# Attention and feed-forward block on one core: a second tile for a unit's finished sums, weight loads placed five slots ahead of their use, and a transposition moved ahead of the weighing

## The chip, the cores and the metric

The kernel runs on one core of a Trainium2 chip. The core has a matmul engine (TensorE, PE in the profile; PEld is its loading of weights), a vector engine (DVE), an activation engine (ScalarE, ACT), GpSimd (POOL) and a queue engine (SyncE, SP) that here issues nearly all transfers. Each works through its own instructions in order and waits on the others by semaphores. The metric is the time of one execution in microseconds (us) on the device; less is better.

## The reference

A pre-normalized attention block and a SwiGLU feed-forward block, in float32, for 2048 tokens of width 640, with 32 heads of 20 and a hidden width of 1728:

```python
qkv = (x @ wqkv).reshape(B, S, 3, H, Dh).transpose(2, 0, 3, 1, 4)   # x: layernormed A_x
scores = jnp.einsum("bhqd,bhkd->bhqk", q, k) * (Dh ** -0.5)
p = softmax(scores, axis=-1)
o = jnp.einsum("bhqk,bhkd->bhqd", p, v)
h = A_x + o.transpose(0, 2, 1, 3).reshape(B, S, D) @ wo
y = layernorm(h)
out = h + (silu(y @ w_gate) * (y @ w_up)) @ w_down
```

## The kernel before

The program has three parts: the projections to queries, keys and values (up to about 324 us in the profile), the attention, and the output projection with the feed-forward. The order of the instructions on each engine is that in which the Python code writes them; a framework adds the semaphores and gives out buffers of named tiles in rotation (`bufs` says how many a tile has). An instruction that writes a tile waits until the last reader of that buffer's former content is done.

The attention is 32 units: 8 groups of 4 heads (g) times 4 chunks of 512 queries (c), `u = 4 * g + c`. Each unit runs over 16 key tiles of 128 keys (`kt`). A step, here also called a slot, is one key tile of one unit; its work is written in the order of the string `ORDER = "WxnSmSsMXs"`:

- `s`, `S`: a product of scores of 128 keys with 512 queries for one head (L1290, PE) and its exponential (L1296, ACT). Four in a step. Their results go through four PSUM banks in turn (`ps_one`).
- `W`: weighing. The probabilities of the key tile two steps back are multiplied with the values (L1300, PE) into the bank `acc`. After the last key tile, `row_sums` copies `acc` into the tile `o` on ACT (L1310), and SP takes the row with the sums of probabilities out of it (`r<-o`, L1313).
- `m`, `M`, `x`, `X`: products of scores for a later unit (L261, L289), of which DVE takes maxima (L267, L298) for that unit's softmax.

The query tile `q_stk` has two rows beside those of each head's queries, into which the negative maximum is written before the unit starts, as a high and a low part; the score product then subtracts it. When the last maximum of unit v is there, DVE puts them together (`neg`, L309) and `closing[v]` is set to two steps later. For most units (`early_end`) the maxima go by way of POOL, DVE and DRAM (`m_d`). For unit 1 and for each last unit of a group (u = 3, 7, ..., 31, called late units here) `max_finish` does it: PE transposes `neg` (L345) into a bank of the `ps_one` rotation, ACT and DVE split it into the tile `m2` (`m` in the profile's names), and SP copies it into the query tile in four transfers (`q_stk<-m`, L352). The last maximum of a late unit comes at key tile 11 of the unit before it, `closing` is key tile 13, and its scores start three steps after that.

The rest of a finished unit is handled in the next one: DVE takes the reciprocal of `r` (L1321) at key tile 4, SP sends it through DRAM (`r_d<-r`, L1323) and spreads it over the partitions (`rb<-r_d`, L1329), POOL scales `o` at key tile 9 (L1335), and SP stores `o` to `o_d` in four transfers at key tile 13 (L1338; 11 in the last group). SP also loads queries three units ahead at key tile 6, the next group's keys in the second unit of a group and its values in the third (L164, L181; at key tiles 8, 10, 12 and 14).

In the `W` of nearly every step (all but key tiles 3 and 4, from unit 1 on) one task of `prepare_weights` is run. It makes the sums and the high and low parts of the feed-forward weights that the third part needs, on POOL, and stores them in DRAM (`w_d`, `d_d`, `j_d`). For a block of weights the tasks are: `load` (SP loads `raw`, L1128 or L1182), empty tasks, `sums` (L1140 to L1145), and pieces (L1108, L1109). Each task, also an empty one, first issues the stores of the piece before it (`store()`, L1099), which wait for POOL. `raw` is two tiles.

Of the kernel before, what the change touches and what calls it, by code (L numbers as in the profile page):

```python
# [9 lines left out]
F32 = mybir.dt.float32  # L10
# [7 lines left out]
P = 128  # L18
# [7 lines left out]
CH = 512  # L26
# [27 lines left out]
def tile_block(ctx: ExitStack, tc: tile.TileContext, x, wqkv, wo, wg, wu, wd, out):  # L54
# [1036 lines left out]
    def prepare_weights():  # L1091


        stores, count = [], [0]

        def store():
            while stores:
                dst, t = stores.pop(0)
                nc.sync.dma_start(dst.bitcast(F32), t.bitcast(F32))  # L1099

        def staged(n):

            count[0] += 1
            t = stages[count[0] % 2][:, count[0] // 2 % 5, : 2 * n]
            return t.rearrange("p (i n) -> p i n", i=2), t

        def part(src, hi, lo):
            nc.gpsimd.tensor_copy(hi, src)  # L1108
            nc.gpsimd.tensor_tensor(out=lo, in0=src, in1=hi.bitcast(F32), op=ALU.subtract)  # L1109

        def nothing():
            store()

        def block(f):

            raw, src = [], {}
            whole = f < NF - 1

            def load():
                store()  # L1120
                for i, m in enumerate((wg, wu)):
                    if whole or i == 0:
                        raw.append(pc.tile([P, ND, P], F32, name="raw", tag="o_t"))
                    if whole:
                        dst, cols = raw[i], m[:, f * P : (f + 1) * P]
                    else:
                        dst, cols = raw[0][:, :, i * LASTW : (i + 1) * LASTW], m[:, f * P :]
                    nc.sync.dma_start(dst, cols.rearrange("(k p) n -> p k n", p=P))  # L1128
                src["A11"], src["A12"] = raw[0][:, 0:2], raw[0][:, 2:4]
                if whole:  # L1130
                    src["A22"] = raw[1][:, 2:4]

            def sums(i):
                store()
                g, u = raw
                t = pc.tile([P, 2, 2, P], F32, name="sums", tag="z2")
                x, y = t[:, 0], t[:, 1]
                tt = nc.gpsimd.tensor_tensor
                if i == 0:
                    tt(out=x, in0=u[:, 0:2], in1=u[:, 2:4], op=ALU.add)  # L1140
                    tt(out=y, in0=x, in1=g[:, 0:2], op=ALU.subtract)
                    src["S1"], src["S2"] = x, y
                else:
                    tt(out=x, in0=g[:, 0:2], in1=u[:, 0:2], op=ALU.subtract)
                    tt(out=y, in0=g[:, 2:4], in1=src["S2"], op=ALU.subtract)  # L1145
                    src["S3"], src["S4"] = x, y

            def unit(kind):
                store()
                t, whole_t = staged(2 * P)  # L1150
                t = t.rearrange("p i (k n) -> p i k n", k=2)
                part(src[kind], t[:, 0], t[:, 1])
                stores.append((w_d[f][:, UNITS.index(kind)], whole_t))

            def last():
                store()
                t = staged(2 * P)[0].rearrange("p i (k n) -> p i k n", k=2)
                for i, r in enumerate(raw):
                    part(r[:, ND - 1], t[:, 0, i], t[:, 1, i])
                n = len(raw)  # L1160
                stores.append((
                    w_d[f][:, 7].rearrange("p (i k n) -> p i k n", i=2, k=2)[:, :, :n], t[:, :, :n]
                ))

            if not whole:
                return [load, nothing, nothing] + [lambda k=k: unit(k) for k in ("A11", "A12")] + [last]
            return (
                [load, nothing, nothing, lambda: sums(0), lambda: sums(1)]
                + [lambda k=k: unit(k) for k in ("A11", "A12")] + [last]
                + [lambda k=k: unit(k) for k in ("A22", "S2", "S1", "S3", "S4")]  # L1170
            )

        def rows(fs, together):

            raw, src = {}, {}

            def load():
                store()
                for f in fs:
                    raw[f] = pc.tile([P, D], F32, name="raw", tag="o_t")  # L1180
                    if f < NF - 1:
                        nc.sync.dma_start(raw[f], wd[f * P : (f + 1) * P, :])  # L1182
                    else:
                        for i in range(2):
                            nc.sync.dma_start(
                                raw[f][i * LASTW : (i + 1) * LASTW, :], wd[f * P :, :]
                            )
                    for i in range(2):
                        src[f, i] = raw[f][:, i * HALF : (i + 1) * HALF]

            def sums(i):
                store()
                b11, b12, b21, b22 = (src[f, k] for f in fs for k in range(2))
                t = pc.tile([P, 2, HALF], F32, name="sums", tag="z2")
                x, y = t[:, 0], t[:, 1]
                tt = nc.gpsimd.tensor_tensor
                if i == 0:
                    tt(out=x, in0=b12, in1=b11, op=ALU.subtract)
                    tt(out=y, in0=b22, in1=x, op=ALU.subtract)
                    src["T1"], src["T2"] = x, y  # L1200
                    src["B11"], src["B21"], src["B22"] = b11, b21, b22
                else:
                    tt(out=x, in0=b22, in1=b12, op=ALU.subtract)
                    tt(out=y, in0=b21, in1=src["T2"], op=ALU.subtract)
                    src["T3"], src["T4"] = x, y

            def piece(name, dst):
                store()
                t, whole = staged(HALF)
                part(src[name], t[:, 0], t[:, 1])  # L1210
                stores.append((dst, whole))

            tasks = [load, nothing, nothing]
            if together:
                tasks += [lambda: sums(0), lambda: sums(1)]
                for i, (_, name, _) in enumerate(SEVEN):
                    tasks.append(lambda i=i, n=name: piece(n, j_d[fs[0] // 2][:, i]))
            else:
                for f in fs:
                    for i in range(2):  # L1220
                        tasks.append(lambda f=f, i=i: piece((f, i), d_d[f][:, i]))
            return tasks

        tasks = []
        for f in range(NF):
            tasks += block(f)
        for f in range(0, NF, 2):
            if f < NF - 2:
                tasks += rows((f, f + 1), True)
            if f in d_d:  # L1230
                tasks += rows((f, f + 1), False)
        return tasks + [store]
# [73 lines left out]
            )  # L1306

    def row_sums(acc, *queues):
        o = pc.tile([P, CH], F32, name="o", bufs=1)
        nc.scalar.activation(o, acc, AF.Copy)  # L1310
        r = pc.tile([P, 16], F32, name="r")
        for j in range(G):
            queues[j % len(queues)].dma_start(  # L1313
                r[32 * j : 32 * j + 32, :],
                o[32 * j + DH : 32 * j + DH + 1, :].rearrange("r (p f) -> r p f", p=32),
            )
        return o, r
# [63 lines left out]
    for u in range(NU):  # L1381
# [4 lines left out]
        for kt in range(NT):  # L1386
# [5 lines left out]
            for op in order:  # L1392
# [7 lines left out]
                elif op in "sS":  # L1400
                    scores(u, kt, heads[op == "S"].pop(0), probs)
                else:
                    if len(todo) == 2:
                        weigh_next()
                    for v, at in closing.items():
                        if at == now[0] and not early_end(v):
                            max_finish(v)
                        elif at == now[0]:
                            store_maxima(v)
                        elif at == now[0] - 3 and early_end(v):  # L1410
                            send_maxima(v)
                    if extra:
                        extra.pop(0)()
                    if preparing and u and kt not in (3, 4):
                        preparing.pop(0)()
                    if now[0] == (NU - NC) * NT + 8:
                        unit_ring, last_ring = weight_rings()
                        unit_ring.fill()
                        last_ring.fill()
            todo.append((u, kt, probs))  # L1420
            if kt == 6 and u + 3 < NU:
                load_queries(u + 3)
            if kt == 10 and u == 0:
# [599 lines left out]
```

## Time and profile before

| | us |
|---|---|
| runs timed (three) | 2020.04, 2023.31, 2024.53; median 2023.31 |
| profiled execution | 2016.94 |
| its span, first to last instruction | 2015.1 |
| granted TensorE clock | 1.00 |

The profiled execution's own time is 1.84 us above its span and 0.3% below the median of the timed runs. In the profile's rows, a line of code is L with its number, `out<-in` are tiles by name, and a bracket at a row's end gives the time that the engine was idle ahead of it and what ended that. Slots of `SPq` are SP issuing a transfer; how long the transfer itself takes is not in that row.

### The profile page before, as it was taken

What the parts mean: (1) busy time and instruction counts of PE and PEld (TensorE: products, weight loads), DVE (VectorE), ACT (ScalarE), POOL (GpSimd) and SP (SyncE); (2) the same over time, 40 slices, a digit from 0 to 9 for tenths busy, and PEclk for the clock granted to TensorE, in tenths of its full rate; (3) what the DMA queues carried; (4) which work ended last, traced back from release to release, by engine and by line L of the source; (5) the groups of instructions that cost most, each with busy time, mean ns of one, the idle gap of its engine ahead of it and who ended that gap; (6) DMA issues with size and microseconds to landing.
All of it is one profiled execution on the core that took longest, in us unless ns stands there. A gap on an engine that the chain in (4) does not pass through costs nothing.

```text
span 2015.1 us, 41996 instructions
## 1 busy us (share of the span) xinstructions
PE 1986.7 (99%) x14792; PEld 1262.6 (63%) x14792; DVE 1607.9 (80%) x2873; ACT 1433.6 (71%) x2833; POOL 782.8 (39%) x1147
## 2 busy tenths in 40 slices
PE   8999999999999999999999999999999999999998
PEld 6989996444344444444444444455588888888888
DVE  5687778999899899999999998975488666676667
ACT  4677778999999999999999999987633222212221
POOL 6564423343352444443500001011155444844455
PEclk9999999999999999999999999999999999999999
DMA  7787563442534544435412122222258655974642
GB/s 237 261 255 253 176 210 86 128 152 93 182 112 126 159 123 145 150 134 183 152 55 73 45 80 58 79 63 62 62 195 286 228 175 171 356 254 158 206 146 93
DMA packets 197066, 310.50 MB, mean 154 GB/s; under 512 B 51368, under 2 KB 85480, under 8 KB 195832
## 3 DMA queue, kind: packets, MB, share of 16 engines
q1 hardware_dynamic: 190264, 284.21, 43.7%
q0 software_dynamic: 6496, 23.60, 4.0%
q8 instruction: 118, 1.93, 0.4%
q14 instruction: 92, 0.75, 0.1%
q10 hardware_dynamic: 96, 0.00, 0.0%
HBM read 208.11 MB, written 99.19 MB: 152 GB/s over the span
## 4 chain that ended last, share of the span: by engine, by line
PE 85%; DMA 4%; DVE 1%; POOL 1%; issue 1%; SPq 1%; ACT 0%; ACTq 0%; POOLq 0%; DVEq 0%
PE acc L1300 23%; PE ps_a L1486 15%; PE ps_one L1290 11%; PE ps_max L289 8%; PE ps_b L1580 8%; PE ps_one L667 6%; PE ps_max L261 6%; PE ps_max L228 2%; PE ps_max L1021 2%; PE ps_b L1021 1%; DMA q_stk<-q_d 1%; DMA halves<-j_d 1%; DMA w_d<-stage 1%; DMA k_stk<-k_d 0%; DMA o_d<-o 0%
## 5 line engine op out<-in xcount | busy, mean ns | idle before, releaser
L1296 ACT ACTIVATE probs<-ps_one 128x512 f32<-128x512 f32 x2048 | 1048.8, 617 | 45.3 <-PE ps_one L1290 33.5
L267 DVE TENSOR_REDUCE found<-ps_max 128x1 f32<-128x512 f32 x980 | 630.7, 685 | 88.6 <-PE ps_max L261 70.5
L1290 PE MATMUL ps_one<-q_stk,k_stk 62*128 62x512 f32 x2048 | 578.6, 428 | 1.1 <-DMA q_stk<-m 0.7
L1300 PE MATMUL acc<-probs,v_stk 128*32 128x512 f32 x4096 | 545.2, 604 | 0.2
L289 PEld LDWEIGHTS ps_max<-k_stk,q_stk 60*128 60x128 f32 x984 | 181.7, 185 | 407.2 <-DVE found L267 390.3
L261 PE MATMUL ps_max<-k_stk,q_stk 60*128 60x512 f32 x980 | 393.2, 422 | 0.0
L298 DVE TENSOR_REDUCE found<-ps_max 128x2 f32<-128x512 f32 x492 | 335.7, 683 | 3.1 <-PE ps_max L289 3.1
L289 PE MATMUL ps_max<-k_stk,q_stk 60*128 60x256 f32 x984 | 324.5, 330 | 4.7 <-ACTq L304 4.6
L1290 PEld LDWEIGHTS ps_one<-q_stk,k_stk 62*128 62x128 f32 x2048 | 303.0, 184 | 26.1 <-ACT probs L1296 21.3
L1701 DVE TENSOR_TENSOR tmp<-ps_a,tmp 128x512 f32<-128x512 f32 x208 | 141.2, 689 | 119.5 <-PE ps_a L1486 93.9
L250 DVE TENSOR_REDUCE mx<-ps_max 128x2 f32<-128x512 f32 x288 | 180.5, 685 | 64.0 <-PE ps_max L228 60.0
L261 PEld LDWEIGHTS ps_max<-k_stk,q_stk 60*128 60x128 f32 x980 | 181.0, 185 | 50.4 <-DVE found L298 23.5
L240 ACT ACTIVATE ps_max<-ps_max 128x512 f32<-128x512 f32 x288 | 151.7, 584 | 46.2 <-PE ps_max L228 43.6
L1580 PE MATMUL ps_b<-halves,yp 128*128 128x320 f32 x1032 | 179.3, 308 | 1.9 <-POOL yp L102 1.2
L1580 PEld LDWEIGHTS ps_b<-halves,yp 128*128 128x128 f32 x1032 | 165.1, 188 | 18.5 <-POOL yp L102 1.5
L1486 PE MATMUL ps_a<-t,units 128*128 128x512 f32 x624 | 162.5, 396 | 0.0
L1300 PEld LDWEIGHTS acc<-probs,v_stk 128*32 128x32 f32 x4096 | 80.6, 108 | 129.4 <-issue 120.7
L1486 PE MATMUL ps_a<-z,units 128*128 128x512 f32 x516 | 133.9, 394 | 0.0
L102 POOL TENSOR_TENSOR yp<-y,yp 128x256 fp32r<-128x256 f32 x96 | 60.2, 627 | 188.0 <-ACT yp L101 180.3
L1486 PEld LDWEIGHTS ps_a<-t,units 128*128 128x128 f32 x624 | 112.6, 188 | 18.5
L1335 POOL TENSOR_TENSOR o<-o,rb 128x512 f32<-128x512 f32 x31 | 39.8, 1285 | 195.6 <-DMA q_stk<-q_d 109.8
L1585 DVE TENSOR_TENSOR h<-ps_b,h 128x320 f32<-128x320 f32 x248 | 110.1, 481 | 7.1 <-PE ps_b L1580 5.6
(220 smaller groups left out, 2975.9 us busy)
## 6 DMA issues: line engine op xcount, KB each, us to landing
units<-w_d SPq DMA_DIRECT2D x186, 256.0 KB
w_d<-stage SPq DMA_DIRECT2D x106, 256.0 KB
halves<-j_d SPq DMA_DIRECT2D x70, 320.0 KB
j_d<-stage SPq DMA_DIRECT2D x42, 320.0 KB
k_stk<-k_d SPq DMA_DIRECT2D x64, 160.0 KB
q_stk<-q_d SPq DMA_DIRECT2D x64, 160.0 KB
raw<-k_d SPq DMA_DIRECT2D x62, 160.0 KB
raw<-q_d SPq DMA_DIRECT2D x54, 160.0 KB
```

What stands on the lines that cost most here:

```text
L240: nc.scalar.activation(ps, ps, AF.Relu)
L250: nc.vector.tensor_reduce(mx[:, b, :, t, kc], ps.rearrange("p (j n) -> p j n", j=2), axis=AX.X, op=ALU.max,)
L261: nc.tensor.matmul(ps, queries[u][rows, pair, t * P : (t + 1) * P], keys[u // NC][rows, pair, kc * CH : (kc + 1) * CH], start=True, stop=True,
L267: nc.vector.tensor_reduce(found_of(u)[:, b, pair, t, kc : kc + 1], ps, axis=AX.X, op=ALU.max)
L289: nc.tensor.matmul(ps[:, b * CH // 2 : (b + 1) * CH // 2], queries[u][rows, pair, t * P : (t + 1) * P], keys[u // NC][rows, pair, first : ...
L298: nc.vector.tensor_reduce(found_of(u)[:, :, pair, t, column], ps.rearrange("p (b n) -> p b n", b=2), axis=AX.X, op=ALU.max,)
L1290: nc.tensor.matmul(ps, keys[u // NC][rows, p, kt * P : (kt + 1) * P], queries[u][rows, p, :], start=True, stop=True,)
L1296: nc.scalar.activation(probs[p][:, b, :], ps, AF.Exp, scale=scale)
L1300: nc.tensor.matmul(acc[32 * j : 32 * j + 32, :], values[u // NC][:, kt, j * VW : j * VW + 32], probs[j // 2][:, j % 2, :], start=(kt == 0) ...
L1486: nc.tensor.matmul(ps.rearrange("p (t n) -> p t n", t=TPC), w[k][:, i], z[k][:, :, j], start=(first and m == 0), stop=(last and m == len(n ...
L1580: nc.tensor.matmul(ps, a, b, start=(n == 0), stop=(n == len(pairs) - 1))
L1701: add = lambda out, ps, x: nc.vector.tensor_tensor(out=out, in0=ps, in1=x, op=ALU.add)
```

## The change

Three edits. `row_sums` gets a second buffer for `o`. In `prepare_weights` each load is followed by four empty tasks instead of two, so the first use of what it loads is five tasks later instead of three; the list grows from 269 to 315 tasks and ends in unit 23 instead of unit 20. And `max_finish` of a late unit is called at the end of the step ahead of `closing`, after that step's last scores, where it was called within the `W` of the step `closing`, after its weighing; it also comes ahead of the loads that stand at that step's end.

```diff
@@ prepare_weights: block, rows
-                return [load, nothing, nothing] + [lambda k=k: unit(k) for k in ("A11", "A12")] + [last]
+                return [load] + [nothing] * 4 + [lambda k=k: unit(k) for k in ("A11", "A12")] + [last]
             return (
-                [load, nothing, nothing, lambda: sums(0), lambda: sums(1)]
+                [load] + [nothing] * 4 + [lambda: sums(0), lambda: sums(1)]
...
-            tasks = [load, nothing, nothing]
+            tasks = [load] + [nothing] * 4
@@ row_sums
-        o = pc.tile([P, CH], F32, name="o", bufs=1)
+        o = pc.tile([P, CH], F32, name="o", bufs=2)
@@ the steps
                     for v, at in closing.items():
-                        if at == now[0] and not early_end(v):
-                            max_finish(v)
-                        elif at == now[0]:
+                        if at == now[0] and early_end(v):
                             store_maxima(v)
...
             todo.append((u, kt, probs))
+            for v, at in closing.items():
+                if at == now[0] + 1 and not early_end(v):
+                    max_finish(v)
             if kt == 6 and u + 3 < NU:
                 load_queries(u + 3)
```

The order on PE around the transposition for unit 3, before. The rows of L1290 are the scores of the running unit, those of L261 and L289 products for later maxima, L1300 the weighing:

```order
L261 MATMUL ps_max<-k_stk_5609,q_stk 128x512
L289 MATMUL ps_max<-k_stk_5609,q_stk 128x256
L1290 MATMUL ps_one<-q_stk,k_stk_145 128x512
L1300 MATMUL acc<-probs,v_stk_146 32x512 x4
L345 MATMUL ps_one<-ident,neg 16x128
L289 MATMUL ps_max<-k_stk_5609,q_stk 128x256
L1290 MATMUL ps_one<-q_stk,k_stk_145 128x512
```

The same place after:

```order
L261 MATMUL ps_max<-k_stk_5609,q_stk 128x512
L289 MATMUL ps_max<-k_stk_5609,q_stk 128x256
L1290 MATMUL ps_one<-q_stk,k_stk_145 128x512
L345 MATMUL ps_one<-ident,neg 16x128
L1300 MATMUL acc<-probs,v_stk_146 32x512 x4
L289 MATMUL ps_max<-k_stk_5609,q_stk 128x256
L1290 MATMUL ps_one<-q_stk,k_stk_145 128x512
```

The transposition (L345) has changed places with the weighing products of one step.

The order on SP in unit 10, from the spreading of the reciprocals to the copies of unit 11's maxima (L352), before. `w_d` are stores of pieces, `raw` loads of weights, `v_stk` loads of values:

```order
L1329 DMA rb<-r_d 128x1x512
L1099 DMA w_d_83<-stage 128x512 x2
L1128 DMA raw<-in_B_w_gate 128x5x128
L1128 DMA raw<-in_B_w_up 128x5x128
L164 DMA q_stk<-q_d_60 40x1024
L164 DMA q_stk<-q_d_60 20x1024
L164 DMA q_stk<-q_d_60 40x1024
L164 DMA q_stk<-q_d_60 20x1024
L181 DMA v_stk_5610<-v_d 128x4x96 x2
L1099 DMA w_d_84<-stage 128x512
L181 DMA v_stk_5610<-v_d 128x4x96
L352 DMA q_stk<-m_11443 1x8x128 x4
```

And after, from the loads of queries on:

```order
L164 DMA q_stk<-q_d_60 20x1024
L1099 DMA w_d_82<-stage 128x512 x2
L181 DMA v_stk_5610<-v_d 128x4x96
L1099 DMA w_d_82<-stage 128x512 x2
L181 DMA v_stk_5610<-v_d 128x4x96
L1099 DMA w_d_82<-stage 128x512
L1128 DMA raw<-in_B_w_gate 128x5x128
L1128 DMA raw<-in_B_w_up 128x5x128
L352 DMA q_stk<-m_11389 1x8x128 x4
L181 DMA v_stk_5610<-v_d 128x4x96
L1338 DMA o_d<-o 20x512 x4
```

Before, the store ahead of the copies (`w_d_84`) is of the block whose load stands a few rows above it. After, all stores ahead of the copies are of a block (`w_d_82`) that was loaded in the unit before; the next block's load stands right ahead of the copies, and one load of values has come behind them.

## The prediction

> **What bounds the kernel now.** I read the page first, then the busy times by stretch, then what ScalarE (ACT) waited for, then the timelines around each wait. The first line is the page's busy times; the second is busy time of the engines in the stretch in which the attention runs undisturbed by other matmuls (PE, PEld, DVE, ACT, POOL in that order, with instruction counts), then the granted clock and the DMA share.
>
> ```profile
> PE 1986.7 (99%) x14792; PEld 1262.6 (63%) x14792; DVE 1607.9 (80%) x2873; ACT 1433.6 (71%) x2833; POOL 782.8 (39%) x1147
> ...
> 328.00:1342.00 1014.00, 1008.18 (x7676) 424.47 (x7672) 919.01 (x1569) 993.11 (x1958) 305.76 (x506) 1.00 0.38 114
> ```
>
> All three edits act between 328 and 1342 us. There ACT is busy 993.11 of 1014 us (98%) and PE's modelled time fills the stretch too: the two run in step, four exponentials against four score products per key tile. ACT works through its instructions in order, so what it idles here nothing gives back. These are all its idle times of 0.4 us or more in the stretch, in the timeline of ACT (start, length, instruction, and in brackets the idle time ahead of it and what ended it):
>
> ```profile
> 529.78 0.60 ACT L1310 ACTIVATE o<-acc 128x512 f32<-128x512 f32 x1 [2.60 <-DMA o_d<-o]
> ...
> 665.52 0.60 ACT L1310 ACTIVATE o<-acc 128x512 f32<-128x512 f32 x1 [1.70 <-DMA w_d<-stage]
> 698.38 2.06 ACT L1296 ACTIVATE probs<-ps_one 128x512 f32<-128x512 f32 x4 [1.14 <-PE ps_max L261]
> 735.31 0.60 ACT L1310 ACTIVATE o<-acc 128x512 f32<-128x512 f32 x1 [1.44 <-DMA o_d<-o]
> ...
> 936.72 0.60 ACT L1310 ACTIVATE o<-acc 128x512 f32<-128x512 f32 x1 [0.43 <-DMA j_d<-stage]
> 969.06 2.06 ACT L1296 ACTIVATE probs<-ps_one 128x512 f32<-128x512 f32 x4 [0.64 <-PE ps_max L261]
> ```
>
> Four are the copy of a unit's sums into `o` (L1310), two the first exponential of a unit. That they are lost for good shows in the distance between these copies, one per unit of 16 key tiles:
>
> ```profile
> 493.60 0.63 ACT L1310 ACTIVATE o<-acc 128x512 f32<-128x512 f32 x1
> ...
> 563.46 0.63 ACT L1310 ACTIVATE o<-acc 128x512 f32<-128x512 f32 x1
> ...
> 596.89 0.63 ACT L1310 ACTIVATE o<-acc 128x512 f32<-128x512 f32 x1
> ```
>
> From 563.46 to 596.89 a unit takes 33.43 us, 2.09 per key tile. From 493.60 to 529.78 it took 36.18, which is 2.75 more and holds the idle 2.60; the next (to 563.46) took 33.68 and recovered nothing.
>
> **Edit 1, two tiles for the finished sums.** With one `o`, the copy for unit u waits until unit u-1's four stores to `o_d` have landed. The stores of the first case, between key loads, in the timeline of SP:
>
> ```profile
> 521.16 2.13 SPq L164 DMA_DIRECT2D k_stk<-k_d  x4
> 523.87 2.95 SPq L1338 DMA_DIRECT2D o_d<-o  x4
> 527.51 1.88 SPq L164 DMA_DIRECT2D k_stk<-k_d  x4
> ```
>
> SP came to the stores only at 523.87, behind a key load, issued the last of them by 526.82, and ACT went on at 529.78. (The other three cases name neighbouring transfers as what ended the wait; it is the same instruction at the same place.) With a second tile the copy needs the stores of u-2, a unit (33.4 us) older, and these were late by at most 2.6. The wait is gone in all four cases: 2.60 + 1.70 + 1.44 + 0.43 = 6.17 us. I take the idle times; the unit's excess of 2.75 against 2.60 says that up to about 0.2 more per case could come back, which I keep for the range. The edit adds no instruction. What is late next in these places is SP's row `r<-o`, behind four key loads: they end at 529.39, and DVE's reciprocals need `r`. For an undisturbed unit:
>
> ```profile
> 426.80 0.63 ACT L1310 ACTIVATE o<-acc 128x512 f32<-128x512 f32 x1
> 427.46 3.42 SPq L1313 DMA_DIRECT2D r<-o  x4
> 435.34 0.24 DVE L1321 RECIPROCAL r<-r 128x16 f32<-128x16 f32 x1
> ```
>
> The reciprocal comes 8.54 us after the copy starts. In unit 5 the copy would start at 527.18, `r<-o` be issued from 529.39 to about 532.8 (3.42, as here), and the reciprocal come at 535.7: 2.9 us are left for the landing. A small copy's landing can be read below as 1.29, so nothing waits.
>
> **Edit 2, loads two slots further ahead.** It adds 46 empty slots, which hold no computing, and moves the preparation's end from unit 20 to unit 23; the weights are read from unit 28 on, so no end moves. Its worth lies in the two first exponentials above. The timelines of POOL, SP and PE for the first (unit 11):
>
> ```profile
> 677.89 0.46 SPq L1128 DMA_DIRECT2D raw<-in_B_w_gate  x1
> ...
> 687.52 0.72 POOL L1140 TENSOR_TENSOR sums<-raw 128x256 f32<-128x256 f32 x1 [18.65 <-DMA raw<-in_B_w_up]
> ...
> 692.86 0.34 SPq L1099 DMA_DIRECT2D w_d<-stage  x1
> 693.24 0.44 SPq L181 DMA_DIRECT2D v_stk<-v_d  x1
> 693.78 2.81 SPq L352 DMA_DIRECT2D q_stk<-m  x4
> 697.88 0.47 PE L1290 MATMUL ps_one<-q_stk,k_stk 62*128 62x512 f32 x1 [0.73 <-DMA q_stk<-m]
> ```
>
> The raw weights took 9.63 us to land (677.89 to 687.52); POOL then made sums, scaled `o` and split the first piece, which SP could store at 692.86: 14.97 us from load to store. The maxima's four copies (L352) stood behind that store. They were issued by 696.59 and the score ran at 697.88, which makes 1.29 us to land; in unit 3, shown below, they start 5.9 us ahead of the score, here 4.1. Before, six slots lie between a load and its first store, 12.5 us at 2.09, and in units 10 and 18 that store stands just ahead of the copies. After, wherever such a store stands ahead of a late unit's copies, at least eight key tiles lie between it and its load (unit 22, whose pieces need no sums; ten in units 2, 14 and 18), 16.7 us: more than 14.97. So both waits go: 1.14 + 0.64 = 1.78 us. Taken at the other end, if they only change place, it is 0. I take 1.78, because eight key tiles cover the longest case. What the loads are moved past: in units 17 to 22 they now stand in key tile 2, on SP behind `r<-o` and ahead of `r_d<-r` and `rb<-r_d`, where their issue costs about 1 us (two of 0.46, by the row above) and their 640 KB travel with `rb`. On POOL the sums that wait for a load now mostly stand behind the scaling of `o` of that unit instead of ahead of it. Both are covered by the room until the scaling's key tile 9, seven key tiles or 14.6 us after the load; if that cover is gone, `o` is stored later, and the second tile hides that.
>
> **Edit 3, the transposition ahead of the weighing.** The late unit 3, which is not disturbed:
>
> ```profile
> 416.29 0.25 DVE L309 TENSOR_REDUCE neg<-found 128x16 f32<-128x96 f32 x1
> ...
> 416.85 1.06 PE L1300 MATMUL acc<-probs,v_stk 128*32 128x512 f32 x8
> ...
> 417.85 0.28 PE L345 MATMUL ps_one<-ident,neg 128*16 128x128 f32 x1
> 418.05 0.38 PE L289 MATMUL ps_max<-k_stk,q_stk 60*128 60x256 f32 x1
> ...
> 418.18 0.25 ACT L101 ACTIVATE m<-ps_one 16x128 fp32r<-16x128 f32 x1
> ...
> 418.45 2.84 SPq L352 DMA_DIRECT2D q_stk<-m  x4
> 418.59 8.36 ACT L1296 ACTIVATE probs<-ps_one 128x512 f32<-128x512 f32 x16 [0.16 <-PE ps_one L1290]
> 424.35 0.49 PE L1290 MATMUL ps_one<-q_stk,k_stk 62*128 62x512 f32 x1
> ```
>
> PE pays 0.2 us for the transposition (417.85 to 418.05) on either side of the eight weighing products, and ACT's copy into `m` stays behind the same four exponentials, so it starts at 418.18 as before. The maximum is ready at 416.54, 0.31 us before PE comes to the place at 416.85. The term is 0; its ends are a gain of the 0.16 that ACT idles at 418.59 and a loss of 0.2, nine times each: -1.4 to +1.8. The margin of the copies is 424.35 - (421.29 + 1.29) = 1.77 us, and one load of values (0.44 at 693.24) now stands behind the copies instead of ahead: good for a backlog, no loss, since those values are for the next group of heads.
>
> **Sum.** -6.17 - 1.78 + 0 = -7.95 us on the profiled execution's 2016.94 gives 2009.0. The three timed runs before have the median 2023.31, 0.3% above the profiled one, so I take the same 7.95 off that: 2015.4.
>
> **Rivals.**
> Rival 1, late units' copies late elsewhere. In unit 10 after the change the raw load (640 KB) stands right ahead of the copies. The nearest case, in unit 6 before:
>
> ```profile
> 549.78 0.45 SPq L1128 DMA_DIRECT2D raw<-in_B_w_gate  x1
> ...
> 555.11 2.82 SPq L352 DMA_DIRECT2D q_stk<-m  x4
> ...
> 556.15 0.74 POOL L1140 TENSOR_TENSOR sums<-raw 128x256 f32<-128x256 f32 x1 [7.41 <-DMA raw<-in_B_w_up]
> 561.01 0.49 PE L1290 MATMUL ps_one<-q_stk,k_stk 62*128 62x512 f32 x1
> ```
>
> The load landed in 6.37 us, during the copies, and PE did not wait. Against it: SP reaches unit 10's load about one key tile later than this one. If again two units wait, edits 2 and 3 bring nothing: 2023.31 - 6.17 = 2017.1. The Trainium skill ("DMA: Bandwidth & Descriptors", section "Queues, rings and completion order") says that each DMA engine takes descriptors of one issuing queue in ring order, so the copies could not pass such a load. By that rule, with a landing of 9.63 us and then the usual 1.29, unit 10's successor would wait about 0.6 us (the load stands two key tiles or 4.4 us ahead of the copies and these 5.9 ahead of the score, 10.3 in all), and the sum would be 2016.0; the case of unit 6, where the load landed in time, neither shows nor excludes it.
>
> Rival 2, no change: the backlog moves to DVE. If `r` lands late, DVE, in order, holds the maxima behind the reciprocal, and PE and ACT follow. For it: SP's backlog itself is not removed by a second tile. Against it: 2.9 us of room above, and these are all of DVE's waits in the stretch, none for `r`:
>
> ```profile
> DVE found L267 <- PE ps_max L261: 68.4, 260, 1.2
> DVE found L298 <- PE ps_max L289: 3.1, 3, 1.7
> DVE h L1027 <- PE ps_max L1021: 2.0, 1, 2.0
> DVE m L102 <- ACT m L101: 0.2, 1, 0.2
> ```
>
> If the four waits came back whole there, only 1.78 would be won: 2021.5.
>
> Rival 3, slower: PE is held at the transposition by the maximum, with the eight weighing products queued behind it, and ACT and DVE starve. It decides when DVE runs later than now by more than 0.31 us; to outweigh 7.95 and reach +0.2% (4.05) it takes 12.0 / 9 = 1.33 us of waiting in each of nine late units. DVE behind by three more of its reductions would make 3 x 0.68 - 0.31 = 1.73 each, 15.6 in all, and 2031.0. Against it: the 68.4 us in which DVE itself waits for PE say that it has room. A reduction's size:
>
> ```profile
> 436.87 0.68 DVE L298 TENSOR_REDUCE found<-ps_max 128x2 f32<-128x512 f32 x1
> ```
>
> **How the numbers follow.** Chances: the forecast 0.62, rival 1 0.19, rival 2 0.13, rival 3 0.06. The forecast and rival 1 (-0.31%) are faster by more than 0.2%, about what a measurement here can tell from no change (the three runs before span 4.5 us); rival 2 (-0.09%) is within it. That gives 0.81, 0.13, 0.06. The range: at the low end the forecast less the kept 0.8 (four times 0.2), less 1.4 for edit 3, and less some 2 for the scatter of a median of runs that span 4.5: 2011. At the high end rival 2: 2021.5. The forecast's own range is 2011 to 2018.
>
> **What the profile after would show.** Right: no idle time ahead of L1310, so that copies of sums stand 33.4 to 33.7 us apart from unit 2 to unit 23; no wait of PE or ACT at the first score of units 11 and 19; the stretch that ends at 1342 now ends about 8 us sooner, with what follows unchanged in length. Wrong: a wait of DVE at L1321, of PE at L345 with the maximum as its end, or a score that waits for `q_stk<-m`. The forecast fails most easily if PE, not ACT, sets the key tile's 2.09 us, so that a freed ACT finds no scores to work on.

## The result, and the profile after

The changed kernel's median is 2009.93 us over six runs, the kernel before's 2022.64 over six; the ratio is 0.9945, with a 95% interval of 0.9927 to 0.9962. A second comparison, further below, gave 0.9958 (0.9944 to 0.9971). The change makes the kernel faster by about half a per cent. The profiled executions are 2016.94 before and 2008.45 after, 8.49 us apart. Two executions of the kernel before, of 3357 and 3631 us, and one of the divided copy below, of 3631 us, ran in a slow state and are left out of the ratios.

All that ACT waited for after the change, between 328 us and the end of the undisturbed attention (1333 us; 1342 before), as who waited for what, total, times, longest:

```profile
ACT probs L1296 <- PE ps_one L1290: 3.1, 13, 0.3
```

The copy L1310 is no longer in this list, and no wait is longer than 0.3 us. The busy times of the stretch (PE, PEld, DVE, ACT, POOL; then the granted clock, the DMA share and GB/s):

```profile
328.00:1333.00 1005.00, 1004.68 (x7667) 423.48 (x7668) 918.62 (x1569) 991.74 (x1956) 305.69 (x506) 1.00 0.38 115
```

ACT's work is what it was (991.74 us, before 993.11 in a stretch cut at slightly other places); its idle time has shrunk, from 20.9 us to 13.3. The timeline of ACT where before had the longest stall:

```profile
493.00 0.63 ACT L1310 ACTIVATE o<-acc 128x512 f32<-128x512 f32 x1
...
526.40 0.63 ACT L1310 ACTIVATE o<-acc 128x512 f32<-128x512 f32 x1
...
560.11 0.63 ACT L1310 ACTIVATE o<-acc 128x512 f32<-128x512 f32 x1
593.53 0.63 ACT L1310 ACTIVATE o<-acc 128x512 f32<-128x512 f32 x1
```

The copies stand 33.40, 33.71 and 33.42 us apart; the 36.18 of before is gone. SP, however, still comes to the stores of `o` in that unit only behind key loads:

```profile
518.75 2.98 SPq L164 DMA_DIRECT2D k_stk<-k_d  x8
522.62 2.01 SPq L1338 DMA_DIRECT2D o_d<-o  x4
```

The last store is issued by 524.63, behind eight key loads, and the copy starts at 526.40, 1.77 us later. Before, 0.36 us lay between them (526.82, and 527.18 for the copy without its wait), so the stores do come somewhat earlier. That alone would not have been enough: in the run with edits 2 and 3 and one tile, below, the same order left ACT waiting 1.13 us at this copy. The second tile makes the landing of these stores irrelevant.

Unit 11, whose first score had waited, in the timelines of SP, POOL and PE:

```profile
681.58 0.45 SPq L1128 DMA_DIRECT2D raw<-in_B_w_gate  x1
682.08 1.07 SPq L1128 DMA_DIRECT2D raw<-in_B_w_up  x1
685.68 2.82 SPq L352 DMA_DIRECT2D q_stk<-m  x4
...
687.67 0.73 POOL L1140 TENSOR_TENSOR sums<-raw 128x256 f32<-128x256 f32 x1 [7.43 <-DMA raw<-in_B_w_up]
691.57 0.49 PE L1290 MATMUL ps_one<-q_stk,k_stk 62*128 62x512 f32 x1
```

The copies go out at 685.68, 5.89 us ahead of the score, as in an undisturbed unit before. The raw load right ahead of them landed in 6.09 us (681.58 to 687.67), and the score did not wait. Last, the transposition of unit 3:

```profile
415.44 0.25 DVE L309 TENSOR_REDUCE neg<-found 128x16 f32<-128x96 f32 x1
...
416.21 0.28 PE L345 MATMUL ps_one<-ident,neg 128*16 128x128 f32 x1
416.42 1.07 PE L1300 MATMUL acc<-probs,v_stk 128*32 128x512 f32 x8
417.41 0.38 PE L289 MATMUL ps_max<-k_stk,q_stk 60*128 60x256 f32 x1
417.48 0.25 ACT L101 ACTIVATE m<-ps_one 16x128 fp32r<-16x128 f32 x1
...
417.94 0.60 ACT L1296 ACTIVATE probs<-ps_one 128x512 f32<-128x512 f32 x1 [0.21 <-PE ps_one L1290]
```

PE transposes 1.2 us ahead of the next key tile's products instead of directly ahead of them, and ACT's copy into `m` still waits its turn behind the exponentials. ACT idles 0.21 us there, before 0.16.

### The profile page after: what moved, and what is told of

It is laid out like the page before. It is cut to its first block, busy times and chain, and to the rows that moved or that the text cites. A ratio compares the mean times of both kernels' runs of the same rounds, so it can differ in the third digit from the quotient of the medians.

```text
span 2006.6 us, 41982 instructions
## 1 busy us (share of the span) xinstructions
PE 1983.5 (99%) x14792; PEld 1261.6 (63%) x14792; DVE 1606.8 (80%) x2873; ACT 1433.0 (71%) x2833; POOL 784.4 (39%) x1147
## 3 DMA queue, kind: packets, MB, share of 16 engines
q8 instruction: 118, 1.93, 0.4%
## 4 chain that ended last, share of the span: by engine, by line
PE 88%; DMA 2%; DVE 1%; POOL 1%; issue 1%; ACT 0%; SPq 0%; DVEq 0%; ACTq 0%; POOLq 0%
PE acc L1300 25%; PE ps_a L1487 15%; PE ps_one L1290 12%; PE ps_max L289 9%; PE ps_b L1581 8%; PE ps_max L261 7%; PE ps_one L667 7%; PE ps_max L228 2%; PE ps_max L1021 2%; PE ps_b L1021 1%; DMA o_t<-o_d 0%; DMA units<-w_d 0%; DMA halves<-j_d 0%; DMA t_d<-kept 0%; PE ps_max L1056 0%
## 5 line engine op out<-in xcount | busy, mean ns | idle before, releaser
L1290 PE MATMUL ps_one<-q_stk,k_stk 62*128 62x512 f32 x2048 | 577.4, 428 | 1.1 <-DVE m L102 0.9
L1300 PE MATMUL acc<-probs,v_stk 128*32 128x512 f32 x4096 | 545.2, 604 | 0.0
L289 PEld LDWEIGHTS ps_max<-k_stk,q_stk 60*128 60x128 f32 x984 | 181.8, 185 | 407.2 <-DVE found L267 400.3
L261 PE MATMUL ps_max<-k_stk,q_stk 60*128 60x512 f32 x980 | 392.7, 422 | 0.0
L289 PE MATMUL ps_max<-k_stk,q_stk 60*128 60x256 f32 x984 | 324.1, 329 | 0.0
L1290 PEld LDWEIGHTS ps_one<-q_stk,k_stk 62*128 62x128 f32 x2048 | 303.1, 184 | 25.3 <-ACT probs L1296 19.5
L261 PEld LDWEIGHTS ps_max<-k_stk,q_stk 60*128 60x128 f32 x980 | 181.0, 185 | 50.2 <-DVE found L298 21.9
L1300 PEld LDWEIGHTS acc<-probs,v_stk 128*32 128x32 f32 x4096 | 80.6, 108 | 127.6 <-issue 118.5
```

Source lines behind the costliest of these rows:

```text
L261: nc.tensor.matmul(ps, queries[u][rows, pair, t * P : (t + 1) * P], keys[u // NC][rows, pair, kc * CH : (kc + 1) * CH], start=True, stop=True,
L289: nc.tensor.matmul(ps[:, b * CH // 2 : (b + 1) * CH // 2], queries[u][rows, pair, t * P : (t + 1) * P], keys[u // NC][rows, pair, first : ...
L1290: nc.tensor.matmul(ps, keys[u // NC][rows, p, kt * P : (kt + 1) * P], queries[u][rows, p, :], start=True, stop=True,)
L1300: nc.tensor.matmul(acc[32 * j : 32 * j + 32, :], values[u // NC][:, kt, j * VW : j * VW + 32], probs[j // 2][:, j % 2, :], start=(kt == 0) ...
```

## The experiments

Each was timed in turn with the kernel before on the same chip. The idle times are those of the run's own profiled execution.

| run | median | before beside it | ratio (95%) |
|---|---|---|---|
| edit 1 alone | 2009.75 | 2020.48 | 0.9951 (0.9938 to 0.9965) |
| edit 2 alone | 2016.04 | 2020.48 | 0.9976 (0.9965 to 0.9986) |
| edit 3 alone | 2020.64 | 2020.48 | 0.9998 (0.9987 to 1.0008) |
| edits 2 and 3 | 2017.33 | 2020.48 | 0.9982 (0.9973 to 0.9990) |
| before again | 2021.50 | 2020.77 | 1.0002 (0.9990 to 1.0013) |
| all, one empty slot | 2015.31 | 2020.77 | 0.9974 (0.9960 to 0.9988) |
| all, copy divided | 2015.00 | 2020.77 | 0.9973 (0.9962 to 0.9984) |
| all, high part on DVE | 2010.83 | 2020.77 | 0.9947 (0.9929 to 0.9965) |
| all, copy on DVE | 2011.35 | 2020.05 | 0.9962 (0.9949 to 0.9974) |
| the change again | 2009.77 | 2020.05 | 0.9958 (0.9944 to 0.9971) |

**The three edits apart.** My theory was that the stalls are separate and each edit takes its own; the rival, that the place of the loads is the root of all of them.

Edit 1 alone:

```diff
-        o = pc.tile([P, CH], F32, name="o", bufs=1)
+        o = pc.tile([P, CH], F32, name="o", bufs=2)
```

> Edit 1 alone: `o` has two tiles, loads and transposition as before. Theory (the stalls are separate, each edit takes its own): the four idle times of ACT ahead of L1310 go, those at the first score of units 11 and 19 stay within about 1 us of 1.14 and 0.64; 6 to 7 us less than before in the profiled execution, ratio about 0.997. Rival (the load's place is the root of all stalls): also no wait at L1310, since the second tile hides it, so this run does not tell the two apart by its time. Rival (the backlog moves to DVE): DVE waits for `r` at L1321 in the same units and the time is within 2 us of before.

All of ACT's waits from 330 us on in this run:

```profile
ACT probs L1296 <- PE ps_max L261: 1.8, 2, 1.2
ACT probs L1296 <- PE ps_one L1290: 1.0, 5, 0.3
```

Nothing waits at L1310, and the two first scores of units 11 and 19 wait their 1.8 us as before. By the list of stalls this is as expected; by the time it is more: 10.7 us between the medians where 6 to 7 were expected. Why is the subject of a part below. (Ahead of 330 us stands one more wait, of 1.45 us, which is also taken up there.)

Edit 2 alone:

```diff
-                [load, nothing, nothing, lambda: sums(0), lambda: sums(1)]
+                [load] + [nothing] * 4 + [lambda: sums(0), lambda: sums(1)]
```

(and the two like it in blocks and rows)

> Edit 2 alone: four empty slots behind each load, one `o` tile, transposition as before. Theory: units 11 and 19 no longer wait for their maxima, but ACT still waits at L1310 wherever SP comes late to the stores of `o`, some 3 to 6 us in all in other units; 1 to 4 us less than before, ratio 0.998 to 0.9995. Rival (the load's place is the root): with sums that never hold POOL, the stores of `o` are in time and nothing waits at L1310; about 8 us less than before, ratio about 0.996, as the full change.

```profile
528.91 0.60 ACT L1310 ACTIVATE o<-acc 128x512 f32<-128x512 f32 x1 [1.55 <-DMA o_d<-o]
664.85 0.60 ACT L1310 ACTIVATE o<-acc 128x512 f32<-128x512 f32 x1 [1.92 <-DMA k_stk<-k_d]
...
1102.82 0.60 ACT L1310 ACTIVATE o<-acc 128x512 f32<-128x512 f32 x1 [0.75 <-PE ps_max L261]
```

These, at the copies of units 5, 9 and 22, are its waits at L1310; the first scores of units 11 and 19 no longer wait. SP in unit 9, ahead of the second:

```profile
655.45 4.01 SPq L164 DMA_DIRECT2D k_stk<-k_d  x8
660.04 1.74 SPq L1338 DMA_DIRECT2D o_d<-o  x4
662.30 1.91 SPq L164 DMA_DIRECT2D k_stk<-k_d  x4
```

Here POOL is not late (in unit 9 it had scaled `o` by 648.28) and the stores of `o` still stand behind eight key loads. So the loads' place is not the root of the waits in units 5 and 9; there it is the order of SP's queue in the second unit of a group. The other two waits at L1310, those of units 11 and 17, do not come in this run, nor in edits 2 and 3 together. For unit 11 the rows of before and of this run show why: before, POOL scaled `o` only at 724.80, behind sums that had waited for their load, and SP came to the stores at 730.35; here POOL scaled it at 717.33 and SP came at 725.18. So the rival is right for that wait and wrong for those of units 5 and 9. The 1.78 us at the first scores and the 1.87 at units 11 and 17 make 3.65 us of the 4.4 between the medians.

Edit 3 alone:

```diff
-                        if at == now[0] and not early_end(v):
-                            max_finish(v)
...
             todo.append((u, kt, probs))
+            for v, at in closing.items():
+                if at == now[0] + 1 and not early_end(v):
+                    max_finish(v)
```

> Edit 3 alone: the late units' maxima transposed ahead of the weighing, one `o` tile, two empty slots. Theory: PE pays its 0.2 us on either side, so all six stalls stay, and the time is that of before within 1.5 us. Because the copies now stand ahead of one load of values, the waits of units 11 and 19 may shrink by up to 0.5 each. Rival (the place of the transposition matters by itself): 3 us or more either way.

The time is that of before within 0.1%. At the first score of unit 11 ACT waits 0.47 us instead of 1.14 and at that of unit 19 no wait is listed, as expected of copies that stand ahead of one load of values. Its waits at L1310 sum to 8.7 us, more than the 6.17 of the execution I had worked from: 6.5 us in units 5, 9 and 17 (3.76, 1.21 and 1.49), none in unit 11, and four of 0.40 to 0.72 at other copies. That not all of the six stalls stayed where they were was not expected.

Edits 2 and 3, the change with one `o` tile:

```diff
-        o = pc.tile([P, CH], F32, name="o", bufs=2)
+        o = pc.tile([P, CH], F32, name="o", bufs=1)
```

> The full change without edit 1: one `o` tile, loads five slots ahead, transposition ahead of the weighing. Theory: as edit 2 alone, 1 to 4 us less than before; ACT waits at L1310 are back, 3 to 6 us in all. Rival (the load's place is the root): as the full change, about 8 us less than before, no wait at L1310.

```profile
ACT o L1310 <- DMA o_d<-o: 3.5, 2, 2.4
ACT o L1310 <- DMA k_stk<-k_d: 3.0, 1, 3.0
```

6.5 us of waiting at L1310 are back, and 7.5 us in time against the full change's medians of 2009.8 to 2009.9, which come from other jobs; by the ratios it is 5 to 7.5. The waits stand in units 5 and 9, and a new one in unit 22:

```profile
1099.38 2.34 SPq L1338 DMA_DIRECT2D o_d<-o  x4
...
1104.64 0.60 ACT L1310 ACTIVATE o<-acc 128x512 f32<-128x512 f32 x1 [2.38 <-DMA o_d<-o]
```

There the moved raw loads (1097.66 to 1099.33) stand right ahead of the stores, which needed until 1104.64 to free the tile. So edit 2 without edit 1 took two of the old waits away, and in both of its runs one came at unit 22, where before had none. Edit 1 carries the change. What edits 2 and 3 add to it is the 1.8 us of waits at the first scores, which lies within the intervals of the timed runs (0.9951 alone, 0.9945 and 0.9958 with them).

**Why the gain is over 8 us.** The kernel before, unchanged:

> The kernel before, unchanged, profiled once more. Theory: the length of ACT's waits at L1310 follows the landing of transfers and differs from one execution to the next; the profiled execution of before, 2016.94, was one of the fastest of its kernel (all runs 2017.1 to 2026.1, median 2020.5), so this profile shows the same places with more than 7.95 us of idle in all, by about as much as its time is above 2017. Rival (the difference between executions lies elsewhere, in the projections or the feed-forward): the idle is again about 8 us and another stretch is longer.

This profiled execution took 2021.22 us, where the first took 2016.94. All of ACT's idle times of 0.4 us or more from 500 to 1000 us:

```profile
531.62 0.60 ACT L1310 ACTIVATE o<-acc 128x512 f32<-128x512 f32 x1 [4.21 <-DMA k_stk<-k_d]
535.15 2.07 ACT L1296 ACTIVATE probs<-ps_one 128x512 f32<-128x512 f32 x4 [0.98 <-PE ps_one L1290]
537.92 20.63 ACT L1296 ACTIVATE probs<-ps_one 128x512 f32<-128x512 f32 x40 [0.71 <-PE ps_one L1290]
...
668.21 0.60 ACT L1310 ACTIVATE o<-acc 128x512 f32<-128x512 f32 x1 [0.83 <-DMA w_d<-stage]
701.01 2.07 ACT L1296 ACTIVATE probs<-ps_one 128x512 f32<-128x512 f32 x4 [1.11 <-PE ps_max L261]
738.12 0.60 ACT L1310 ACTIVATE o<-acc 128x512 f32<-128x512 f32 x1 [1.63 <-DMA o_d<-o]
940.21 0.60 ACT L1310 ACTIVATE o<-acc 128x512 f32<-128x512 f32 x1 [1.07 <-DMA j_d<-stage]
972.81 2.07 ACT L1296 ACTIVATE probs<-ps_one 128x512 f32<-128x512 f32 x4 [0.89 <-PE ps_max L261]
```

The six places are the same six. They sum to 9.74 us, where the first execution had 7.95: the waits were 1.79 us longer. The two idle times that follow the longest within 7 us, 1.69 us together, are of another kind. The busy times there (PE, PEld, DVE, ACT, POOL; then the granted TensorE clock) and two of PE's weighings:

```profile
533.00:535.00 2.00, 2.00 (x12) 0.68 (x6) 0.04 (x1) 1.17 (x3) 1.84 (x6) 0.50 0.07 15
537.00:539.00 2.00, 2.00 (x24) 0.92 (x16) 1.25 (x3) 1.29 (x4) 1.84 (x5) 1.00 0.12 45
...
532.46 1.93 PE L1300 MATMUL acc<-probs,v_stk 128*32 128x512 f32 x8
538.40 1.06 PE L1300 MATMUL acc<-probs,v_stk 128*32 128x512 f32 x8
```

The granted clock fell to 0.50 at about 530 us, while PE stood still because ACT waited, and was back at 1.00 by 537. In between, the eight products of a weighing took 1.93 us instead of 1.06, and ACT waited for scores. From copy to copy this unit took 35.43 us (531.62 to 567.05); the first execution, whose clock stayed at 1.00 behind its wait of 2.60, took 33.68 there. So a wait can cost a second time after it has ended. The third difference is an idle time of 1.33 us at 328 us, at the attention's start, where the granted clock was also 0.50. It comes with two tiles too: the run of edit 1 alone has one like it, 1.45 us at a clock of 0.53. (The three sum to 4.81 us and not to the 4.28 between the two executions, since the second began its attention 1.2 us sooner.)

The rest of the gain in the timed runs goes along with the clock. Of the 73 executions of the kernel before in the experiments, only nine had a mean granted clock of 0.999 or 1.000, with a median of 2017.0 us; the other 64, at 0.993 to 0.998, have 2020.8. Of the changed kernel's eleven, nine had 0.999 or 1.000, with a median of 2009.5. At that clock the two kernels are 7.6 us apart, close to the list of stalls. Taken by tiles, 15 of 106 executions with one `o` tile (before, edit 2, edit 3, edits 2 and 3) reach that clock, and 13 of 16 with two (edit 1 alone, the change); where edit 1 was timed in turn with the kernel before, it was four of 5 against one of 27. How much of the difference is the clock itself, and how much longer waits in the same executions, the times alone do not tell.

So the theory holds in part: the waits do differ from one execution to the next, but longer waits are less than half of the difference between the two profiled executions. The rival, that another stretch is longer, has the 1.33 us at the attention's start for it. What neither named is the granted clock. What makes it fall is not settled here. A stretch at 0.50 follows waits at L1310 of 4.21 us (before again), 3.76 (edit 3), 2.95 (edits 2 and 3) and 1.92 (edit 2), but not those of 2.60 (before) and 2.38 (edits 2 and 3); and some executions, with one tile and with two, have one at about 325 or 1380 us, where no copy of sums waits.

**The changed kernel again.**

> The changed kernel, unchanged, profiled once more, in the same job as runs of before. Theory: no wait of ACT at L1310 and none at a late unit's first score in this execution either, since a unit's stores now have 33 us more and the copies stand behind old stores only; time 2008 to 2012, ratio 0.994 to 0.996. Rival (the first profile was a lucky execution): one or more of the six places show again 0.4 us or more.

```profile
ACT probs L1296 <- PE ps_one L1290: 3.3, 14, 0.3
```

As in the first profile of after: no wait over 0.3 us. The rival, a lucky execution, falls for these two profiles.

**What the empty slots are worth.**

```diff
-                [load] + [nothing] * 4 + [lambda: sums(0), lambda: sums(1)]
+                [load] + [nothing] * 1 + [lambda: sums(0), lambda: sums(1)]
```

(and the two like it)

> The changed kernel with one empty slot behind each load instead of four; two `o` tiles and the moved transposition stay. Theory: the store ahead of a late unit's copies now stands five key tiles (10.4 us) behind its load where such a store comes, less than the 14.97 us that it took in unit 10, so one to three late units wait for their maxima, 1 to 3 us each, and no wait stands at L1310: 2 to 5 us more than the full change, ratio to before 0.996 to 0.998. Rival (the slots are worth nothing once `o` has two tiles): as the full change, ratio 0.995.

The size came out, about 5.4 us above the full change (2015.31 against 2009.9, from another job; ratio 0.9974), but the place did not: no late unit waits for its maxima. DVE waits:

```profile
DVE turned L329 <- POOL both L320: 2.2, 3, 1.0
DVE r L1321 <- DMA r<-o: 1.9, 1, 1.9
DVE r L1321 <- DMA w_d<-stage: 0.9, 1, 0.9
```

The longest, in the timelines of POOL, SP, ACT and DVE:

```profile
930.46 0.45 POOL L1108 CAST stage<-raw 128x320 fp32r<-128x320 f32 x1 [12.57 <-DMA raw<-in_B_w_down]
...
931.30 0.63 ACT L1310 ACTIVATE o<-acc 128x512 f32<-128x512 f32 x1
...
935.43 0.82 SPq L1099 DMA_DIRECT2D d_d<-stage  x2
936.34 2.98 SPq L1313 DMA_DIRECT2D r<-o  x4
941.77 0.25 DVE L1321 RECIPROCAL r<-r 128x16 f32<-128x16 f32 x1 [1.86 <-DMA r<-o]
943.15 2.21 ACT L1296 ACTIVATE probs<-ps_one 128x512 f32<-128x512 f32 x4 [1.07 <-PE ps_one L1290]
```

POOL gets its weights only at 930.46, SP waits with the stores of pieces, and `r<-o` goes out 5.04 us after the copy that it needs (936.34 against 931.30; 0.66 in the unit that the prediction quotes). DVE stands at the reciprocal for 1.86 us, and ACT idles 1.07 and, in the next 7 us, 1.30 and 0.69, the latter two at a granted clock that was 0.50 from about 944.8 to 948.3. This is the mechanism of rival 2, and also its cousin at L329, where DVE waits for POOL's part of a unit's maxima. They cost the four-slot kernel nothing: neither stands in its lists of waits. The run compares one slot with four; that the old two slots would do with a second tile, but for 1.8 us of waits, is what edit 1 alone shows.

**What the copy and the transposition still cost.** With no stall left, PE still idles at each unit's first weighing until ACT has copied (7.4 us in 29 waits after). Three attempts at that and at the transposition.

```diff
-        nc.scalar.activation(o, acc, AF.Copy)
+        nc.scalar.activation(o[:, : CH // 2], acc[:, : CH // 2], AF.Copy)
+        nc.vector.tensor_copy(o[:, CH // 2 :], acc[:, CH // 2 :])
```

> The changed kernel with the copy of finished sums divided: ACT copies 256 columns and DVE the other 256 (L1310). It measures what the copy still costs where nothing waits: PE idles up to 0.3 us at each unit's first weighing until ACT has copied. Theory (ACT and PE together set the pace, DVE has room: it waits 63.5 us for PE in the stretch): 0.1 to 0.25 us less per unit, 3 to 8 us less than the full change. Rival (DVE sets the pace as much): the 0.35 us that DVE works more per unit come back in full, 0 to 10 us more than the full change.

```profile
DVE o L1311 <- ACT o L1310: 10.8, 29, 0.6
...
PEld acc L1300 <- DVE o L1311: 14.3, 29, 0.5
```

DVE's half waited for ACT's, so the halves ran one after the other and PE's loading of weights waited 14.3 us instead of 7.4. Why it waited was not looked into. The run does not measure a division side by side; as it stands it is 5 us slower than the full change.

```diff
-        nc.scalar.activation(o, acc, AF.Copy)
+        nc.vector.tensor_copy(o, acc)
```

> The changed kernel with the whole copy of finished sums on DVE instead of ACT (L1310). In the run with a copy divided between the two, DVE's half waited for ACT's half (10.8 us in 29 waits), so that run did not measure the division. Theory (PE and ACT set the pace, DVE has 51.9 to 63.5 us in which it waits for PE): the copy, about 0.65 us, fits into DVE's waits, and each of 29 units loses up to 0.3 us of PE's wait for ACT's copy: 0 to 8 us less than the full change. Rival (DVE's queue is as full as PE's at the place where the copy stands): the copy comes later on DVE than it does on ACT, PE waits for it with the bank of the next unit's sums, 0.2 us and more per unit, 5 us or more above the full change.

```profile
PEld acc L1300 <- DVE o L1310: 8.7, 29, 0.3
```

2011.35 against 2009.77 for the changed kernel in the same job: no gain, by the medians 1.6 us of loss, within the two intervals. ACT is freed of 0.63 us per unit and PE still waits 0.3. The theory's range came down to its end of 0, and the rival's 5 us or more did not come. What can be said is that freeing ACT of this copy does not shorten a unit.

```diff
-        split(m, parts[:, 0], parts[:, 1], nc.vector)
+        nc.vector.tensor_copy(parts[:, 0], m)
+        nc.vector.tensor_tensor(out=parts[:, 1], in0=m, in1=parts[:, 0].bitcast(F32), op=ALU.subtract)
```

> The changed kernel with the high part of a late unit's transposed maxima copied by DVE instead of ACT. It measures what a transposition still costs: ACT idles 0.21 us and works 0.25 us for each of nine. Theory (PE's 0.2 us are the cost, ACT's copy fits into the time that PE takes): no more than 1 us less than the full change, within the scatter. Rival (ACT's copy is the cost): 0.25 to 0.45 us less for each of nine, 2 to 4 us less.

2010.83, ratio 0.9947: the full change within the scatter, as the theory had it.

## Why the prediction was right, and where not

*Edit 1.* The mechanism and the places held: the waits at L1310 are gone in both profiles of after and in edit 1 alone, are back in edits 2 and 3 together, and nothing took their place at the reciprocal. The size is the term that was too small. I put it at 6.17 us from one execution; the same places give 7.74 in the second execution of before (4.21 + 0.83 + 1.63 + 1.07), with 1.69 more in the idle times that follow the longest, at half the clock. Timed, edit 1 alone is worth 0.49% (0.35 to 0.62), 10 us. The remark that the older stores "were late by at most 2.6" was also too small, though without harm: a unit is 33.4 us.

*Edit 2.* Both waits of late units went, as in edit 2 alone. 1.78 was taken, 2.00 stood in the second execution of before. What I had not put down is that the old places of the loads also cause two of the four waits at L1310, those of units 11 and 17: alone, the edit won 4.4 us by the medians. The two edits overlap there, and with a second tile in place this part has nothing left to win.

*Edit 3.* A term of 0 was right: ratio 0.9998 alone, 0.21 us of idle instead of 0.16 at ACT.

*The sum.* In the profiled executions 7.95 was forecast and 8.49 came. That these two agree so well is partly luck: both happened to run at a granted clock of 1.00. Against the median the same 7.95 gave 2015.4; the medians came out at 2009.93 and 2009.77. The step that failed is the one from profile to median: I saw that the profiled execution stood 0.3% below the median, and took the same amount off both. The 6.4 us between the two before consist of longer waits (1.79 us between the two profiled executions) and of time at half the granted clock, part of it right behind such waits (1.69) and part at the attention's start (1.33). The sum has no term for the clock. The second tile raises it as well: at 0.999 and above the kernels are 7.6 us apart, over all executions 10 to 13. So both medians lie about 1 us under the range's low end of 2011; by the ratio, on the median that I worked from, it is 2012.2 (2023.31 x 0.9945). My allowance of 2 us for scatter looked on the slow end of before's executions as noise.

*The rivals.* Rival 1 did not come: no late unit waits after, and the raw load ahead of unit 11's copies had landed (687.67) before SP had issued the last of them (688.50). The rule of the Trainium skill on ring order ("DMA: Bandwidth & Descriptors", section "Queues, rings and completion order"), by which I had put that unit's wait at 0.6 us, could not show: the load took 6.09 us here, not 9.63. That the copies could not pass the load was moreover my inference: the section gives the order in which descriptors are taken, and adds that a later one may finish its write before an earlier one. Rival 2 did not come with four slots, but the run with one slot shows that its mechanism is real. Rival 3 did not come: the maximum was ready at 415.69 in unit 3, PE transposed at 416.21 without a wait. That PE and not ACT sets the pace, which I named as the likeliest failure, fits one run: taking 0.63 us per unit from ACT won nothing. But that did not keep a freed ACT from going on, because both had stood still together in the stalls (PE idled 2.23 us in the one of 2.60).

## What to carry to other kernels

A wait for a buffer behind a queue of transfers has no fixed length here, and the granted clock may fall behind it: before costing its removal, take two or three profiled executions, and list the granted clock of every timed one beside its time. A gap between profile and median may be either. Where one queue served stores that free a buffer and loads that are needed later, a second buffer was worth more than moving the loads, because the order of the queue no longer mattered. And slots between a load and its first use were worth something only up to the point where the in-order engine behind them was no longer late; with fewer, look for where the backlog comes out, which may be another engine than the one that waited.

## What was not expected of the hardware

The same transfers in the same order let ACT wait 2.60 us in one execution and 4.21 in another at the same instruction (unit 5, before), with the stores of `o` issued by 526.82 in the one and by 528.20 in the other. Measured from where the copy would have started, the last store was issued 0.36 us ahead in the first and 0.79 behind in the second, and the landing took 2.96 and 3.42: 1.15 and 0.46 make the 1.61 us, so it is the issue that varied, more than the landing. Issuing the four stores took 3.11 us in the second and 2.95 in the first, so SP had fallen behind earlier, at the key loads ahead of them (517.25 in the first, 518.62 in the second). The rows of the second:

```profile
525.09 3.11 SPq L1338 DMA_DIRECT2D o_d<-o  x4
528.87 1.92 SPq L164 DMA_DIRECT2D k_stk<-k_d  x4
```

And the granted clock can halve behind a wait of a few microseconds, in one execution and not in the next of the same program, so that the wait is paid for again.
